# Softmax denominators of a local-attention kernel: a column of ones in the value tile and a vector shuffle in place of matmuls with ones

## Chip, cores, metric

The kernel runs on one core of a Trainium2 chip. The metric is the device time of one execution in microseconds (us); smaller is better. Before the change it was 201.92 us (median of 3 runs, 201.13 to 202.17).

Engines by their short names: PE is TensorE (matmuls), ACT is ScalarE (activation functions), DVE is VectorE, POOL is GpSimd.

## The reference, cut to what matters

```python
xn = _layernorm(x)                                # x: 1 x 2048 x 448, bf16
# attention over 16 heads of 28, window of 8 keys at distance 0, 2, ... 14
q, k, v = split(xn @ wqkv)
logits = einsum("bhsd,bhswd->bhsw", q, gather(k)) * 28 ** -0.5    # masked where the key lies before 0
attn = softmax(logits, axis=-1)
s = reshape(einsum("bhsw,bhswd->bhsd", attn, gather(v))) @ wo
# feed-forward on the same xn, hidden width 1792
g = silu(gelu(xn @ w1 + b1) @ w2 + b2)
return x + s * g
```

## The kernel before

Even and odd positions are handled as two sequences, which makes the window contiguous. Positions are cut into blocks of 121 queries with 128 keys. A *unit* is four blocks of one group of four heads. There are four stages `c = 0..3` of 512 positions; each has an FFN part (`ffn1_pair`) and then an attention part with four units (five in the last stage). The attention part also does the second FFN matmul of the stage (`ps_y`) and, in all but the last stage, the projections q, k and v of the next stage: that is work with which PE fills the time while a unit passes through the other engines.

```python
vw = [big.tile([P, H, 32], BF16) ...]       # per block: keys x heads x 32; 28 columns of v, 4 zero columns

def qk_unit(c, i):                          # logits of a unit, exp, mask
    ...
    for j, (g, b) in enumerate(u):
        for h in range(4):
            nc.tensor.matmul(Sp[h // 2][:, h % 2, j, 0:QW], kT[...], qT[...], start=True, stop=True)
    for p2 in range(2):
        ev = E[:, 2 * p2:2 * p2 + 2, :, 0:QW]
        nc.scalar.activation(ev, Sp[p2][:, :, :, 0:QW], ACT.Exp, scale=SCALE)
        nc.vector.tensor_tensor(out=ev, in0=ev, in1=mk..., op=ALU.mult)
    return E

def av_unit(c, i, E):                       # denominators, numerators, quotient
    psO = psB.tile([P, 4, P], F32, name="psO", tag="B")
    psD = psB.tile([P, 4, P], F32, name="psD", tag="B")
    for h in range(4):                      # denominators: 32 columns of ones, so that all 32 rows hold the sum
        nc.tensor.matmul(psD[32 * h:32 * h + 32, :, 0:QW], ones[:, :], E[:, h, :, 0:QW], start=True, stop=True)
    for j, (g, b) in enumerate(u):          # numerators
        for h in range(4):
            nc.tensor.matmul(psO[32 * h:32 * h + 32, j, 0:QW], vw[b][:, 4 * g + h, :], E[:, h, j, 0:QW],
                             start=True, stop=True)
    nc.scalar.activation(ld[:, :, 0:n], psD[:, :, 0:n], ACT.Ln)                  # 1/den as exp(-ln(den))
    nc.scalar.activation(R[:, :, 0:n], ld[:, :, 0:n], ACT.Exp, scale=-1.0)
    nc.vector.tensor_tensor(out=dst, in0=psO[:, :, 0:n], in1=R[:, :, 0:n], op=ALU.mult)   # -> oT

# order of the program; PE and ACT run exactly in this order, DVE is ordered by a scheduler
for c in range(NC):
    for k in range(MT // 2):
        ffn1_pair(c, 2 * k)                 # ps_h, then gelu on ACT, two at a time, in 2 PSUM tiles (psA)
        ...                                 # silu and output projection of earlier rows, transposes
    jobs = iter(list(qkv_jobs(c + 1))) if c + 1 < NC else iter(())
    n_units = 4 + (c == 3)
    for i in range(n_units):
        E = qk_unit(c, i)
        if i < 4:
            ffn2_job(4 * c + i)             # ps_y, then y = ps_y + b2 on DVE
        run(jobs, 3 if i < 3 else 99)       # none in the last stage
        av_unit(c, i, E)
...                                         # tail: tanh, silu, last output projections
```

The logits tiles `S` and the `ps_h` tiles share two PSUM tiles (psA); `ps_y`, `ps_qk`, `ps_v`, `psO`, `psD` and others share four PSUM buffers in rotation (psB).

The softmax here doesn't subtract the row's maximum and nothing guards it: scores larger than these inputs give would overflow.

Of the kernel before, what the change touches and what calls it, by code (L numbers as in the profile page):

```python
# [8 lines left out]
F32 = mybir.dt.float32  # L9
BF16 = mybir.dt.bfloat16  # L10
U32 = mybir.dt.uint32
ALU = mybir.AluOpType
ACT = mybir.ActivationFunctionType
ENG = mybir.EngineType

S, D, H, DH, F = 2048, 448, 16, 28, 1792
P = 128
# [6 lines left out]
QB = 121  # L24
QW = 122
# [8 lines left out]
def kernel(  # L34
# [14 lines left out]
    nc = tc.nc  # L49
# [8 lines left out]
    const = ctx.enter_context(tc.tile_pool(name="const", bufs=1))  # L58
    big = ctx.enter_context(tc.tile_pool(name="big", bufs=1))
    work = ctx.enter_context(tc.tile_pool(name="work", bufs=2))  # L60
    psA = ctx.enter_context(tc.tile_pool(name="psA", bufs=2, space=bass.MemoryType.PSUM))
    psB = ctx.enter_context(tc.tile_pool(name="psB", bufs=4, space=bass.MemoryType.PSUM))
# [6 lines left out]
    vw = [big.tile([P, H, 32], BF16, name=f"vw_{b}") for b in range(NB)]  # L69
# [8 lines left out]
    wo = big.tile([P, 4, D], BF16, name="wo")  # L78
# [2 lines left out]
    lnv = const.tile([P, NT], F32, name="lnv")  # L81
    ident = const.tile([P, P], BF16, name="ident")
    eps_t = const.tile([P, 1], F32, name="eps_t")
    ones = const.tile([P, 32], BF16, name="ones")
    b1t = const.tile([P, MT], BF16, name="b1t")
    b1f = const.tile([P, MT], F32, name="b1f")
    b2bc = const.tile([P, D], BF16, name="b2bc")
# [33 lines left out]
        nc.gpsimd.memset(tl[:, :, 0:LEAD].bitcast(U32), 0)  # L121
        nc.gpsimd.memset(tl[:, :, LEAD + S:LQ].bitcast(U32), 0)
    nc.gpsimd.memset(w1[64:128, 3, :].bitcast(U32), 0)
    nc.gpsimd.memset(ones[:], 1.0)
    for b in range(NB):
        nc.gpsimd.memset(vw[b][:, :, DH:32].bitcast(U32), 0)

    nc.gpsimd.memset(mk_gen[:, :, :], 1.0)
    nc.gpsimd.affine_select(out=mk_gen[:, :, :], in_=mk_gen[:, :, :], compare_op=ALU.is_ge, fill=0.0,
# [12 lines left out]
    for g in range(4):  # L142
        for h in range(4):
            r = (4 * g + h) * DH
            nc.gpsimd.dma_start(wo[32 * h:32 * h + DH, g, :], A_wo[r:r + DH, :])
    nc.gpsimd.tensor_copy(b1f[:], b1t[:])


# [34 lines left out]
    def v_job(b):  # L183
        ps = psB.tile([P, D], F32, name="ps_v", tag="B")
        o = LEAD + QB * b - 7
        for kt in range(KT):
            nc.tensor.matmul(ps[:, :], xnT[:, kt, o:o + P], wqkv[:, kt, 2 * D:3 * D],  # L187
                             start=(kt == 0), stop=(kt == KT - 1))
        nc.scalar.copy(vw[b][:, :, 0:DH], ps[:, :].rearrange("p (h c) -> p h c", h=H))  # L189

    def ffn1_pair(c, m0):
        ps = psA.tile([P, 2, CH], F32, name="ps_h", tag="A")
# [36 lines left out]
    def unit(c, i):  # L229
        if i < 4:  # L230
            return [(i, 4 * c + j) for j in range(4)]
        return [(g, NB - 1) for g in range(4)]

    def qk_unit(c, i):
        u = unit(c, i)
        E = work.tile([P, 4, 4, P], BF16, name="E", tag="E", bufs=2)
        Sp = [psA.tile([P, 2, 4, P], F32, name="S", tag="A") for _ in range(2)]
        for j, (g, b) in enumerate(u):
            o = LEAD + QB * b
            for h in range(4):  # L240
                r = slice(32 * h, 32 * h + DH)
                nc.tensor.matmul(Sp[h // 2][:, h % 2, j, 0:QW], kT[r, g, o - 7:o - 7 + P],  # L242
                                 qT[r, g, o:o + QW], start=True, stop=True)
# [3 lines that stand above are left out]
            mk = mk_gen if i == 4 or c % 2 else (mk_0, None, mk_8)[c]  # L247
            nc.vector.tensor_tensor(out=ev, in0=ev,  # L248
                                    in1=mk[:, :, :].unsqueeze(1).to_broadcast((P, 2, 4, QW)), op=ALU.mult)
        return E  # L250

    def av_unit(c, i, E):
        u = unit(c, i)
        psO = psB.tile([P, 4, P], F32, name="psO", tag="B")
        psD = psB.tile([P, 4, P], F32, name="psD", tag="B")
        for h in range(4):
            nc.tensor.matmul(psD[32 * h:32 * h + 32, :, 0:QW], ones[:, :], E[:, h, :, 0:QW],  # L257
                             start=True, stop=True)
        for j, (g, b) in enumerate(u):
            for h in range(4):  # L260
                nc.tensor.matmul(psO[32 * h:32 * h + 32, j, 0:QW], vw[b][:, 4 * g + h, :],  # L261
                                 E[:, h, j, 0:QW], start=True, stop=True)
        n = QB if i < 4 else S - QB * (NB - 1)
        ld = work.tile([P, 4, QB], F32, name="ld", tag="ld", bufs=2)
        R = work.tile([P, 4, QB], F32, name="R", tag="R", bufs=2)
        nc.scalar.activation(ld[:, :, 0:n], psD[:, :, 0:n], ACT.Ln)  # L266
        nc.scalar.activation(R[:, :, 0:n], ld[:, :, 0:n], ACT.Exp, scale=-1.0)  # L267
        if i < 4:
            dst = oT[:, i, 4 * QB * c:4 * QB * (c + 1)].rearrange("p (j q) -> p j q", j=4)
        else:  # L270
            dst = oT[:, :, QB * (NB - 1):S]
        nc.vector.tensor_tensor(out=dst, in0=psO[:, :, 0:n], in1=R[:, :, 0:n], op=ALU.mult)  # L272
# [3 lines left out]
    def qkv_jobs(c):  # L276
        for g in range(4):
            for which in range(2):
                yield lambda g=g, which=which: qk_job(c, g, which)
        for b in range(4 * c, 4 * c + 4 + (c == 3)):  # L280
            yield lambda b=b: v_job(b)
# [9 lines left out]
    with tc.manual_schedule(engines={ENG.PE, ENG.Activation}):  # L291
# [13 lines left out]
        for c in range(NC):  # L305
# [23 lines left out]
# [3 lines that stand above are left out]
                    ffn2_job(4 * c + i)  # L332
                run(jobs, 3 if i < 3 else 99)
                if i == 4:
                    pass
                av_unit(c, i, E)
# [36 lines left out]
```

## Time and profile before

| | before |
|---|---|
| time, median | 201.92 us |
| busy: PE, DVE, ACT | 172.6, 111.8, 117.3 of 201.3 us |
| lengths of stages 1 to 4 (see below) | 41.19, 41.95, 42.19, 23.53 us |
| last stage, from one ld to the next | 4.13 us |

How to read the stage lengths: in the timeline of ACT, every FFN part ends with a gelu pair in front of a load of the exp table. The length of a stage is the time from the start of that last gelu pair to that of the next; the fourth runs from the last such pair to the table load in front of the closing tanh. So a stage here is an attention part with the FFN part that follows it, and the fourth is the last attention part alone. The two gelu pairs that bound the first stage of the kernel before (timeline of ACT: start us, length us, engine and line, operation; in brackets the idle time before it and what ended it):

```profile
41.95 1.26 ACT L201 ACTIVATE hT<-ps_h,b1f 128x512 bf16<-128x512 f32 x2 [0.46 <-PE ps_h L196]
...
83.14 1.26 ACT L201 ACTIVATE hT<-ps_h,b1f 128x512 bf16<-128x512 f32 x2 [0.46 <-PE ps_h L196]
```

The first stage is 83.14 - 41.95 = 41.19 us long.

The busy line of the page of the kernel before, engine by engine: busy us, share of the span, number of instructions.

```profile
PE 172.6 (86%) x1384; PEld 84.1 (42%) x1384; DVE 111.8 (56%) x220; ACT 117.3 (58%) x181; POOL 16.0 (8%) x56
```

PE is busiest, but not everywhere the limit. Two pieces of the chain of waits of the kernel before (start us, length us, engine, what); the first piece is from the first stage, the second from the last stage:

```profile
49.01 0.32 PE psD L257 x4
49.32 0.21 PE psO L261 x16
...
171.75 0.68 DVE E L248
172.43 0.04 issue
172.48 0.40 PE psD L257 x2
172.90 0.58 ACT ld L266
173.50 0.61 ACT R L267
174.11 1.76 ACT E L246 x2
```

In the first stage one PE item follows another: PE is the chain, and psD is 0.32 us of it per unit. In the last stage, where no projections are left to fill PE's time, the chain goes round a ring: mask multiply, psD, ld, R, the next unit's exps. ACT runs in the order of the program, so the exps of unit i+1 stand behind ld and R of unit i, and PE and DVE wait in turn.

The groups of instructions that the change concerns, kernel before: line, engine, operation, output and inputs, shapes, count; then busy us in total and mean ns of one; then the engine's idle time just before them and what ended it:

```profile
L272 DVE TENSOR_TENSOR oT<-psO,R 128x484 bf16<-128x484 f32 x16 | 10.6, 662 | 24.5 <-ACT R L267 24.5
...
L267 ACT ACTIVATE R<-ld 128x484 f32<-128x484 f32 x16 | 9.7, 606 | 0.5
...
L266 ACT ACTIVATE ld<-psD 128x484 f32<-128x484 f32 x16 | 9.2, 576 | 22.6 <-PE psD L257 22.6
...
L257 PE MATMUL psD<-E,ones 128*32 128x488 bf16 x68 | 8.7, 384 | 3.6 <-DVE E L248 3.2
...
L261 PE MATMUL psO<-E,vw 128*32 128x122 bf16 x272 | 8.0, 222 | 0.0
```

The oT multiply is the model for a shuffle's cost: the same 484 fp32 elements per partition, read from PSUM by DVE in 662 ns. The timeline of the kernel before, in the form explained above. The first two lines are ACT and PE at the start of the second FFN part, the others ACT in the last stage:

```profile
70.21 1.26 ACT L201 ACTIVATE hT<-ps_h,b1f 128x512 bf16<-128x512 f32 x2
...
71.59 1.89 PE L196 MATMUL ps_h<-xnT,w 128*128 128x512 bf16 x8
...
172.90 0.57 ACT L266 ACTIVATE ld<-psD 128x484 f32<-128x484 f32 x1 [1.17 <-PE psD L257]
...
177.03 0.57 ACT L266 ACTIVATE ld<-psD 128x484 f32<-128x484 f32 x1 [1.18 <-PE psD L257]
```

The first gelu pair ends at 70.21 + 1.26 = 71.47 us, and the third ps_h pair, which needs the PSUM tile that this gelu frees, starts at 71.59 us. PE could not have come much earlier with profit. In the last stage ld starts every 177.03 - 172.90 = 4.13 us.

### The profile page before, as it was taken

The page shows a single profiled execution, that of the slowest core. Times are in us where ns is not written, and L with a number is a line of the kernel's source. Part 1 is how long each engine was busy: PE and PEld are TensorE (multiplying, and loading weights), DVE is VectorE, ACT ScalarE, POOL GpSimd, SP SyncE. Part 2 cuts the span into 40 slices and gives each one's busy share as a digit, 9 for nine tenths or more (in the row PEclk, how much of TensorE's full clock was granted, in tenths as well). Part 3 has the DMA queues.
Part 4 walks back from the last instruction along what each step waited for, and adds up shares of the span by engine and source line. Part 5 has one row for each costly group of instructions (what it writes and reads, how often), then busy time and mean ns, then how long its engine had stood idle before and what let it go on. Part 6 is the DMA issues. An engine that isn't in the chain of part 4 may idle for free.

```text
span 201.3 us, 3396 instructions
## 1 busy us (share of the span) xinstructions
PE 172.6 (86%) x1384; PEld 84.1 (42%) x1384; DVE 111.8 (56%) x220; ACT 117.3 (58%) x181; POOL 16.0 (8%) x56
## 2 busy tenths in 40 slices
PE   0048999979999999799999998899999997998570
PEld 0032445434455454345454543454444443444230
DVE  1886794009775356087753464377651651665494
ACT  0600057684356895745567965754469857657750
POOL 8966000000000000000000000000000000000000
PEclk9999999999999999999999999999999999999787
DMA  5999900000000001000000002000000010000002
GB/s 186 359 229 276 295 2 3 0 0 0 3 0 3 2 0 46 26 0 0 3 0 3 0 23 68 0 5 0 3 0 0 23 49 23 0 3 2 3 23 91
DMA packets 9743, 8.82 MB, mean 44 GB/s; under 512 B 2592, under 2 KB 8832, under 8 KB 9728
## 3 DMA queue, kind: packets, MB, share of 16 engines
q1 hardware_dynamic: 8704, 7.00, 12.4%
q10 hardware_dynamic: 512, 1.20, 1.6%
q0 software_dynamic: 512, 0.40, 1.0%
q8 instruction: 11, 0.18, 0.4%
q14 instruction: 4, 0.03, 0.0%
HBM read 6.77 MB, written 1.84 MB: 43 GB/s over the span
## 4 chain that ended last, share of the span: by engine, by line
PE 73%; ACT 11%; DMA 6%; DVE 6%; issue 2%; DVEq 0%
PE ps_h L196 23%; PE ps_y L207 16%; PE ps_qk L177 15%; PE ps_v L187 6%; DMA wqkv<-in_A_wqkv_dram 6%; PE ps_s L220 5%; ACT E L246 5%; ACT hT L201 3%; PE psD L257 3%; PE S L242 2%; DVE E L248 2%; PE psO L261 2%; ACT ld L266 1%; PE pT L165 1%; DVE sg L223 1%
## 5 line engine op out<-in xcount | busy, mean ns | idle before, releaser
L196 PE MATMUL ps_h<-xnT,w 128*128 128x512 bf16 x224 | 52.3, 379 | 0.2 <-ACT hT L201 0.2
L207 PE MATMUL ps_y<-w,hT 128*128 128x448 bf16 x224 | 45.2, 353 | 0.0
L201 ACT ACTIVATE hT<-ps_h,b1f 128x512 bf16<-128x512 f32 x56 | 35.4, 684 | 15.6 <-PE ps_h L196 15.5
L177 PE MATMUL ps_qk<-xnT,wqk 128*128 128x512 bf16 x128 | 32.1, 406 | 1.9 <-DVE xnT L166 1.9
L246 ACT ACTIVATE E<-S 128x976 bf16<-128x976 f32 x34 | 31.3, 973 | 0.0
L196 PEld LDWEIGHTS <-w 128*128 128x128 bf16 x224 | 21.3, 98 | 23.9 <-issue 0.5
L207 PEld LDWEIGHTS <-hT 128*128 128x128 bf16 x224 | 20.6, 98 | 19.2
L272 DVE TENSOR_TENSOR oT<-psO,R 128x484 bf16<-128x484 f32 (+1 forms) x17 | 11.2, 659 | 26.4 <-ACT R L267 26.4
L266 ACT ACTIVATE ld<-psD 128x484 f32<-128x484 f32 (+1 forms) x17 | 9.8, 574 | 24.0 <-PE psD L257 24.0
L189 ACT CAST vw<-ps_v 128x448 bf16<-128x448 f32 x17 | 9.0, 532 | 23.0 <-PE ps_v L187 23.0
L177 PEld LDWEIGHTS <-wqk 128*128 128x128 bf16 x128 | 13.1, 103 | 18.7 <-issue 3.8
L165 PE MATMUL pT<-ident,xnb 128*128 128x128 bf16 x64 | 6.7, 242 | 12.0 <-DVE xnb L159 12.0
L248 DVE TENSOR_TENSOR E<-E,mk_gen 128x976 bf16<-128x976 bf16 x18 | 12.0, 669 | 7.4 <-ACT E L246 7.4
L220 PE MATMUL ps_s<-wo,oT 128*128 128x448 bf16 x64 | 15.3, 376 | 0.0
L214 DVE SCALAR_TENSOR_TENSOR g<-th,y 128x448 bf16<-128x448 bf16 x16 | 9.8, 624 | 8.8 <-ACT th L213 8.7
L248 DVE TENSOR_TENSOR E<-E,mk 128x976 bf16<-128x976 bf16 x16 | 10.7, 668 | 7.0 <-ACT E L246 6.8
L187 PE MATMUL ps_v<-wqkv,xnT 128*128 128x448 bf16 x68 | 14.0, 352 | 0.0
L223 DVE SCALAR_TENSOR_TENSOR sg<-ps_s,g 128x448 bf16<-128x448 f32 x16 | 9.9, 622 | 7.0 <-PE ps_s L220 7.0
L159 DVE TENSOR_SCALAR xnb<-x,mv,rstd 128x448 bf16<-128x448 bf16 x16 | 5.7, 389 | 13.5 <-ACT rstd L156 13.5
L181 DVE CAST qT<-ps_qk 128x512 bf16<-128x512 f32 x16 | 11.0, 687 | 2.7 <-PE ps_qk L177 2.7
L181 DVE CAST kT<-ps_qk 128x512 bf16<-128x512 f32 x16 | 11.0, 689 | 2.1 <-PE ps_qk L177 2.0
L151 DVE BATCH_NORM_STATS2 st<-x 128x6 f32<-128x448 bf16 x16 | 9.5, 606 | 4.2 <-DMA x<-in_A_x_dram 4.2
(49 smaller groups left out, 136.2 us busy)
## 6 DMA issues: line engine op xcount, KB each, us to landing
out_dram<-o_t SPq DMA_DIRECT2D x16, 112.0 KB, 1.7
w<-in_B_w_dram SPq DMA_DIRECT2D x1, 1568.0 KB, 15.8
x<-in_A_x_dram SPq DMA_DIRECT2D x3, 448.0 KB, 8.7
w<-in_B_w_dram SPq DMA_DIRECT2D x1, 1344.0 KB, 10.3
wqkv<-in_A_wqkv_dram ACTq DMA_DIRECT2D x3, 336.0 KB, 4.5
x<-in_A_x_dram SPq DMA_DIRECT2D x4, 112.0 KB, 4.2
wo<-in_A_wo_dram POOLq DMA_DIRECT2D x16, 24.5 KB, 6.1
w<-in_B_w_dram SPq DMA_DIRECT2D x1, 224.0 KB, 10.3
```

Source lines behind the costliest of these rows:

```text
L177: nc.tensor.matmul(ps[:, :], wqk[:, kt, 16 * which + 4 * g:16 * which + 4 * g + 4, :], xnT[:, kt, LEAD + c * CH:LEAD + (c + 1) * CH], star ...
L181: nc.vector.tensor_copy(dst[:, g, LEAD + c * CH:LEAD + (c + 1) * CH], ps[:, :])
L187: nc.tensor.matmul(ps[:, :], xnT[:, kt, o:o + P], wqkv[:, kt, 2 * D:3 * D], start=(kt == 0), stop=(kt == KT - 1))
L196: nc.tensor.matmul(ps[:, i, :], w1[:, kt, m * P:(m + 1) * P], xnT[:, kt, LEAD + c * CH:LEAD + (c + 1) * CH], start=(kt == 0), stop=(kt == ...
L201: nc.scalar.activation(hT[0][:, m, :], ps[:, i, :], ACT.Gelu_apprx_tanh, bias=b1f[:, m:m + 1])
L207: nc.tensor.matmul(ps[:, :], hT[0][:, m, tt * P:(tt + 1) * P], w2[:, m, :], start=(m == 0), stop=(m == MT - 1))
L220: nc.tensor.matmul(ps[:, :], oT[:, g, t * P:(t + 1) * P], wo[:, g, :], start=(g == 0), stop=(g == 3))
L223: nc.vector.scalar_tensor_tensor(out=sg[:], in0=ps[:, :], scalar=0.5, in1=g_sb[t % 8][:], op0=ALU.mult, op1=ALU.mult)
L246: nc.scalar.activation(ev, Sp[p2][:, :, :, 0:QW], ACT.Exp, scale=SCALE)
L248: nc.vector.tensor_tensor(out=ev, in0=ev, in1=mk[:, :, :].unsqueeze(1).to_broadcast((P, 2, 4, QW)), op=ALU.mult)
L266: nc.scalar.activation(ld[:, :, 0:n], psD[:, :, 0:n], ACT.Ln)
L272: nc.vector.tensor_tensor(out=dst, in0=psO[:, :, 0:n], in1=R[:, :, 0:n], op=ALU.mult)
```

## The change

The intent: the padded value tile has four unused columns per head. If one of them holds ones, the numerator matmul yields the denominator as one of its 32 rows for nothing, and 68 matmuls with ones fall away. But the denominator then stands in one row, and the division needs it in all 32. DVE's stream shuffle, called with the selection `[0] * 32`, copies row 0 of each group of 32 rows to all 32. The column of ones is put first, so v, and the rows of wo that go with it, move by one.

```diff
-    ones = const.tile([P, 32], BF16, name="ones")
...
-    nc.gpsimd.memset(ones[:], 1.0)
     for b in range(NB):
-        nc.gpsimd.memset(vw[b][:, :, DH:32].bitcast(U32), 0)
+
+        nc.gpsimd.memset(vw[b][:, :, 0:1], 1.0)
+        nc.gpsimd.memset(vw[b][:, :, DH + 1:32], 0.0)
...
-            nc.gpsimd.dma_start(wo[32 * h:32 * h + DH, g, :], A_wo[r:r + DH, :])
+            nc.gpsimd.dma_start(wo[32 * h + 1:32 * h + 1 + DH, g, :], A_wo[r:r + DH, :])
...
-        nc.scalar.copy(vw[b][:, :, 0:DH], ps[:, :].rearrange("p (h c) -> p h c", h=H))
+        nc.scalar.copy(vw[b][:, :, 1:DH + 1], ps[:, :].rearrange("p (h c) -> p h c", h=H))
...
         psO = psB.tile([P, 4, P], F32, name="psO", tag="B")
-        psD = psB.tile([P, 4, P], F32, name="psD", tag="B")
-        for h in range(4):
-            nc.tensor.matmul(psD[32 * h:32 * h + 32, :, 0:QW], ones[:, :], E[:, h, :, 0:QW],
-                             start=True, stop=True)
...
-        nc.scalar.activation(ld[:, :, 0:n], psD[:, :, 0:n], ACT.Ln)
+        den = work.tile([P, 4, QB], F32, name="den", tag="den", bufs=2)
+        nc.vector.stream_shuffle(den[:, :, 0:n], psO[:, :, 0:n], [0] * 32)
+        nc.scalar.activation(ld[:, :, 0:n], den[:, :, 0:n], ACT.Ln)
```

## The prediction

> **What bounds the kernel now.** TensorE (PE) is busy 172.6 of 201.3 us, VectorE (DVE) 111.8, ScalarE (ACT) 117.3 (the page's busy times); the limit changes with the stage. In the chain of waits, PE is the chain in the first three attention stages (43 to 152 us): each unit adds 0.32 us of psD and 0.21 us of psO matmuls to it. At each following FFN stage the third pair of ps_h matmuls waits for ACT: in the timeline the first gelu pair ends at 71.47 us and the third matmul pair starts at 71.59: 0.1 us of slack; after the third attention stage ACT is the chain outright (vw, ld, R, table load, gelu from 151.1 to 155.4). In the last attention stage (168 to 190 us) the chain is a loop of 4.13 us per unit: two exps E 1.76, mask multiply 0.68, psD 0.42, ld 0.58, R 0.61, next exps.
>
> **What changes.** Removed: 68 psD matmuls; psO starts 0.21 us after psD in the timeline, so PE gains about 0.2 us per unit. Added: 17 shuffles on DVE, reading 484 fp32 elements from PSUM. [...] The oT multiply of this shape and source takes 0.66 us in the trace, so I estimate 0.66 to 0.77 us each, about 12 us of DVE work. Moved: ld now waits psO, then the shuffle, not psD; it reads SBUF, not PSUM (R from SBUF takes 606 ns, ld 576: +0.03 us). The value tiles' memsets double on GpSimd, long before use: no cost.
>
> **On the critical path.**
> - First three stages: PE gets about 0.2 x 4 = 0.8 us ahead per stage, but the last unit's ld now follows psO and a shuffle. By the timeline it still starts at about 67.7 us; R, table load and first gelu keep their times, and the third ps_h pair waits for them. The gain turns into a PE wait on gelu of about 0.7 us. DVE, saturated around 48 to 50 us, takes 0.7 us more per 6 us unit; masks come late in places: +0.0 to +0.3 us per stage. Together +0.3.
> - Last stage: shuffle plus hand-over enters the loop, 4.13 becoming about 4.9 to 5.1 us. Four units give +3.2 to +4.0, the fifth (448 elements, no new exps) +0.7 to +0.9. Together +4.3.
> - Tail only shifts.
>
> **Predicted time: 206.5 us, range 204.3 to 208.8 (8 in 10).** Faster by over 2%: 0.01; within: 0.37; slower: 0.62.
>
> **What would show it.** PE busy down by roughly 10 us; shuffle group x17 at 0.66 to 0.77 us; DVE busy near 123 us. In the last stage the E pairs 4.9 to 5.1 us apart instead of 4.13, ld waiting on den instead of psD (24.0 us in the waits); and a new wait of PE ps_h on ACT hT of about 0.7 us at each FFN stage's third pair. The first three stages keep their length within 0.3 us.
>
> **What would make it wrong.** A shuffle far from 0.7 us (at 0.4 us the result is within 2%). The psD matmuls costing PE more than 0.2 us per unit, while the FFN stage doesn't wait for gelu: then up to 2.5 us come back. DVE lateness of the masks compounding in stages one to three: slower than the range.

(The sum: 201.9 + 0.3 + 4.3 = 206.5 us. Of the estimate for one shuffle, the lower end, 0.66 us, is the oT multiply of the trace; the upper end, 0.77 us, was the author's estimate, which no trace showed. "Saturated" stands for 1.91 us of DVE work in the 2.00 us from 48 to 50 us of the kernel before.)

## The result, and the profile after

| | before | after |
|---|---|---|
| time, median (range) | 202.04 us (201.13 to 202.31, 4 runs) | 206.75 us (206.40 to 207.25, 4 runs) |
| stage 1 | 41.19 | 41.65 |
| stage 2 | 41.95 | 42.39 |
| stage 3 | 42.19 | 42.64 |
| stage 4 | 23.53 | 27.38 |
| last stage, from one ld to the next | 4.13 | 4.91 |

The ratio is 1.0243 (95% interval 1.0204 to 1.0282): slower by 2.4%. A ratio here is the mean time of one kernel's fast runs over the mean time of the other's fast runs of the same rounds, so it is not quite the ratio of the medians quoted.

The stages grew by 0.46 + 0.44 + 0.45 + 3.85 = 5.20 us in the two profiled executions; the medians differ by 4.71 us. The profiled execution of before happened to have a late start: its first stage began at 41.95 us, that of the changed kernel at 40.73 us. A second profile of the unchanged kernel (below) began it at 39.77 us with the same stage lengths, so this gap belongs to the execution and not to the change. The first stage of the changed kernel lies between these two gelu pairs, 82.38 - 40.73 = 41.65 us:

```profile
40.73 1.27 ACT L201 ACTIVATE hT<-ps_h,b1f 128x512 bf16<-128x512 f32 x2 [0.46 <-PE ps_h L196]
...
82.38 1.27 ACT L201 ACTIVATE hT<-ps_h,b1f 128x512 bf16<-128x512 f32 x2 [0.46 <-PE ps_h L196]
```

The busy line of the page, changed kernel:

```profile
PE 167.9 (82%) x1299; PEld 82.4 (40%) x1316; DVE 121.6 (59%) x254; ACT 117.9 (57%) x181; POOL 17.7 (9%) x72
```

PE fell by 4.7 us and DVE rose by 9.8 us; neither number is the answer. (The trace has 1299 matmul records where it should have 1316, 68 fewer than before; the others are missing from the record, which makes PE's fall look larger than it is.)

One round of the ring in the last stage, in the chain of waits of the changed kernel:

```profile
171.88 0.67 DVE E L248
172.55 0.50 DVE y L209
173.05 0.69 DVE den L263
173.76 0.61 ACT ld L264
174.40 0.61 ACT R L265
175.01 1.75 ACT E L246 x2
```

The shuffle (den) stands between the numerators and ld. In this round the psO matmuls finish under the cover of the y addition, which DVE does meanwhile, so they don't appear; den, the shuffle, adds its whole length. The groups, changed kernel, in the form shown above (its lines are numbered differently: psO is L257 here):

```profile
L263 DVE STREAM_SHUFFLE den<-psO 128x484 f32<-128x484 f32 x16 | 11.1, 695 | 0.0
...
L264 ACT ACTIVATE ld<-den 128x484 f32<-128x484 f32 x16 | 9.7, 606 | 35.2 <-DVE den L263 35.2
...
L257 PE MATMUL psO<-E,vw 128*32 128x122 bf16 x272 | 8.3, 224 | 8.7 <-DVE E L248 8.1 <-DVE y L209 0.7
```

A shuffle takes 695 ns, 33 ns more than the oT multiply of the same shape, and ld takes 606 ns in place of 576 now that it reads SBUF (R, which reads SBUF at the same shape, takes 606 ns in both kernels). The waits of the changed kernel (engine and what waited, for whom: us in total, times, longest us):

```profile
ACT ld L264 <- DVE den L263: 37.3, 17, 4.0
...
PE psO L257 <- DVE E L248: 8.1, 9, 3.3
...
PE ps_h L196 <- ACT hT L201: 2.4, 3, 1.1
...
PE psO L257 <- DVE y L209: 0.7, 2, 0.3
```

The 24.0 us that ld waited for psD before have become 37.3 us of waiting for den. PE, the busiest engine, now waits on DVE for masks (8.1 us, against 3.2 us in front of psD before; all of it in the last stage) and for y (0.7 us), and on ACT's gelu (2.4 us at three places, 0.2 us at one place before). The timeline of the changed kernel; the first two lines are PE around the end of the first stage, then three of DVE ahead of it, then ACT in the last stage:

```profile
65.78 0.40 PE L257 MATMUL psO<-E,vw 128*32 128x122 bf16 x16 [0.33 <-DVE y L209]
...
70.83 1.89 PE L196 MATMUL ps_h<-xnT,w 128*128 128x512 bf16 x8 [0.65 <-ACT hT L201]
...
60.77 0.70 DVE L263 STREAM_SHUFFLE den<-psO 128x484 f32<-128x484 f32 x1
...
64.53 0.67 DVE L248 TENSOR_TENSOR E<-E,mk 128x976 bf16<-128x976 bf16 x1 [0.20 <-ACT E L246]
65.11 0.62 DVE L209 TENSOR_TENSOR y<-ps_y,b2bc 128x448 f32<-128x448 f32 x1
...
173.76 0.61 ACT L264 ACTIVATE ld<-den 128x484 f32<-128x484 f32 x1 [1.92 <-DVE den L263]
...
178.68 0.61 ACT L264 ACTIVATE ld<-den 128x484 f32<-128x484 f32 x1 [1.92 <-DVE den L263]
```

The last unit's psO of the first stage waits 0.33 us for y, and the third ps_h pair waits 0.65 us for gelu. In the last stage ld starts every 178.68 - 173.76 = 4.92 us, and ACT's idle time in front of ld is 1.92 us in place of 1.17.

### The profile page after: what moved, and what is told of

Its sections match the earlier page's. It is cut to its first block, busy times and chain, and to the rows that moved or that the text cites. A ratio compares the mean times of both kernels' runs of the same rounds, so it can differ in the third digit from the quotient of the medians.

```text
span 205.0 us, 3274 instructions
## 1 busy us (share of the span) xinstructions
PE 167.9 (82%) x1299; PEld 82.4 (40%) x1316; DVE 121.6 (59%) x254; ACT 117.9 (57%) x181; POOL 17.7 (9%) x72
## 4 chain that ended last, share of the span: by engine, by line
PE 34%; ACT 29%; DVE 29%; issue 4%; DMA 2%; SPq 0%; DVEq 0%
PE ps_h L196 19%; ACT E L246 9%; DVE den L263 6%; PE ps_qk L177 6%; DVE E L248 5%; ACT ld L264 5%; ACT R L265 5%; ACT hT L201 4%; PE ps_s L220 4%; DVE y L209 4%; DVE qT L181 3%; DVE kT L181 3%; DMA x<-in_A_x_dram 2%; PE ps_v L187 2%; ACT L320 2%
## 5 line engine op out<-in xcount | busy, mean ns | idle before, releaser
L196 PE MATMUL ps_h<-xnT,w 128*128 128x512 bf16 x216 | 51.5, 379 | 2.9 <-ACT hT L201 2.4
L177 PE MATMUL ps_qk<-xnT,wqk 128*128 128x512 bf16 x119 | 30.7, 399 | 2.3 <-DVE xnT L166 1.9
L264 ACT ACTIVATE ld<-den 128x484 f32<-128x484 f32 (+1 forms) x17 | 10.3, 605 | 37.3 <-DVE den L263 37.3
L220 PE MATMUL ps_s<-wo,oT 128*128 128x448 bf16 x64 | 16.2, 393 | 0.0
L257 PE MATMUL psO<-E,vw 128*32 128x122 bf16 x272 | 8.3, 224 | 8.7 <-DVE E L248 8.1
```

What stands on the lines that cost most here:

```text
L177: nc.tensor.matmul(ps[:, :], wqk[:, kt, 16 * which + 4 * g:16 * which + 4 * g + 4, :], xnT[:, kt, LEAD + c * CH:LEAD + (c + 1) * CH], star ...
L196: nc.tensor.matmul(ps[:, i, :], w1[:, kt, m * P:(m + 1) * P], xnT[:, kt, LEAD + c * CH:LEAD + (c + 1) * CH], start=(kt == 0), stop=(kt == ...
L220: nc.tensor.matmul(ps[:, :], oT[:, g, t * P:(t + 1) * P], wo[:, g, :], start=(g == 0), stop=(g == 3))
L264: nc.scalar.activation(ld[:, :, 0:n], den[:, :, 0:n], ACT.Ln)
```

## Experiments

The theory to test: the shuffle costs as *latency*, wherever a chain of dependent steps runs through it (the ring of the last stage, and the end of each earlier stage). The rival: it costs as *occupancy* of DVE, which is about 10 us busier, wherever it stands. All kernels gave the right result except the one that is wrong on purpose. Kernels of one heading ran on the same chip and share the runs of the kernel before. Stage lengths of all runs, us:

| kernel | ratio to before (95%) | stage 1 | 2 | 3 | 4 |
|---|---|---|---|---|---|
| before | 1 | 41.19 | 41.95 | 42.19 | 23.53 |
| changed | 1.0243 (1.0204 to 1.0282) | 41.65 | 42.39 | 42.64 | 27.38 |
| before_again | 0.9985 (0.9948 to 1.0022) | 41.19 | 41.95 | 42.20 | 23.52 |
| shuffle_first3 | 1.0071 (1.0041 to 1.0100) | 41.65 | 42.39 | 42.64 | 23.52 |
| shuffle_last | 1.0168 (1.0143 to 1.0193) | 41.19 | 41.95 | 42.19 | 27.38 |
| dead_shuffle | 1.0003 (0.9973 to 1.0033) | 41.20 | 41.95 | 42.19 | 23.53 |
| no_den (wrong) | 0.9930 (0.9898 to 0.9962) | 40.60 | 41.36 | 41.66 | 24.01 |
| shuffle_unit3 | 1.0102 (1.0058 to 1.0146) | 41.81 | 42.56 | 42.87 | 23.32 |
| shuffle_units012 | 0.9975 (0.9934 to 1.0017) | 41.05 | 41.78 | 41.96 | 23.53 |
| pipe_before | 0.9827 (0.9791 to 0.9863) | 41.20 | 41.95 | 42.19 | 20.37 |
| pipe_after | 0.9923 (0.9887 to 0.9960) | 41.64 | 42.39 | 42.64 | 21.05 |
| ahead_before | 0.9991 (0.9953 to 1.0030) | 42.39 | 43.15 | 42.59 | 20.57 |
| ahead_after | 0.9843 (0.9808 to 0.9878) | 41.20 | 41.95 | 41.39 | 21.06 |
| combined | 0.9668 (0.9625 to 0.9711) | 40.37 | 41.13 | 41.00 | 19.75 |

The stage lengths repeat to 0.01 us from one execution to the next (before and before_again; the one exception is the fourth stage of shuffle_unit3, explained there), which makes them a far sharper instrument than the total time.

### Where the loss sits: four kernels on one chip

**before_again.** The kernel before, unchanged (no edit).

> The kernel before, unchanged, as a control: ratio 1.00 within 0.3%. Its profile is to show how far the start-up varies: the last gelu pair of the first FFN stage began at 41.95 us in the profile of before and at 40.73 in that of the changed kernel. If that 1.2 us belongs to the single execution and not to the change, this run can show a value near 41 as well; if it stays at 41.95, the change itself shortened the start-up.

Measured: 201.45 us, ratio 0.9985; the last gelu pair of the first FFN part began at 39.77 us, the stage lengths are those of before. The start-up varies with the execution and says nothing about the change.

**shuffle_first3 and shuffle_last.** The layout of the changed kernel throughout, and in each stage one or the other source of the denominators:

```diff
         psO = psB.tile([P, 4, P], F32, name="psO", tag="B")
+        shuffled = c < 3                 # shuffle_last: c == 3
+        if not shuffled:
+            psD = ...                    # and the four matmuls with ones, as before
...
+        if shuffled:
             nc.vector.stream_shuffle(den[:, :, 0:n], psO[:, :, 0:n], [0] * 32)
             nc.scalar.activation(ld[:, :, 0:n], den[:, :, 0:n], ACT.Ln)
+        else:
+            nc.scalar.activation(ld[:, :, 0:n], psD[:, :, 0:n], ACT.Ln)
```

> Shuffle in the first three attention stages, matmuls with ones in the last. Latency theory (the shuffle costs where it stands in a chain of dependent steps): the last stage's loop is back at 4.13 us per unit, the first three stages keep their +0.45 us each, so before + 1.35 us, about 203.3 us, ratio 1.005 to 1.008. Rival, occupancy of VectorE (each shuffle costs its share of the 4.7 us wherever it stands): 12 of 17 shuffles, so +3.3 us, about 205.3 us, ratio 1.016.

Measured: 203.58 us, ratio 1.0071; the first three stages as in the changed kernel, the fourth as in the kernel before. The timeline of ACT in its last stage:

```profile
173.71 0.57 ACT L275 ACTIVATE ld<-psD 128x484 f32<-128x484 f32 x1 [1.17 <-PE psD L261]
...
177.85 0.57 ACT L275 ACTIVATE ld<-psD 128x484 f32<-128x484 f32 x1 [1.18 <-PE psD L261]
```

From one ld to the next 4.14 us, and the idle time before ld is back at 1.17 us.

> Matmuls with ones in the first three attention stages, shuffle in the last alone. Latency theory: loop of 4.91 us per unit in the last stage, the first three as before, so +3.7 to +3.9 us, about 205.8 us, ratio 1.018 to 1.020. Occupancy rival: 5 of 17 shuffles, so +1.4 us, about 203.4 us, ratio 1.007.

Measured: 205.17 us, ratio 1.0168, a little under the expected 1.018, which lies inside the interval. The fourth stage is that of the changed kernel, 27.38 us. Its timeline there:

```profile
171.98 0.61 ACT L273 ACTIVATE ld<-den 128x484 f32<-128x484 f32 x1 [1.92 <-DVE den L272]
...
176.89 0.61 ACT L273 ACTIVATE ld<-den 128x484 f32<-128x484 f32 x1 [1.92 <-DVE den L272]
```

What follows: the two losses are separate and add up (0.71% + 1.68% = 2.39% against 2.43%). Five shuffles of the last stage cost 3.85 us, twelve of the first three 1.35 us. Per shuffle that is 0.77 us against 0.11 us, so the cost goes by place and not by number. The occupancy rival had expected the opposite proportion. (The 0.11 us are net of what PE gains in these stages; no_den, below, puts that gain at 1.71 us, and (1.35 + 1.71) / 12 = 0.26 us is then the price of a shuffle there. In the last stage no_den finds no gain to set off.)

**dead_shuffle.** The kernel before, with the same 17 shuffles added, but nobody reads them:

```diff
+        den = work.tile([P, 4, QB], F32, name="den", tag="den", bufs=2)
+        nc.vector.stream_shuffle(den[:, :, 0:n], psO[:, :, 0:n], [0] * 32)
         nc.scalar.activation(ld[:, :, 0:n], psD[:, :, 0:n], ACT.Ln)
```

> The kernel before with all 17 shuffles added, their result read by nobody; the denominators still come from matmuls with ones. Latency theory: VectorE is as busy as in the changed kernel (about 122 us), but no step waits for the shuffle, so the last stage's loop stays at 4.13 to 4.3 us and the time at 202.0 to 203.0 us, ratio 1.000 to 1.005. Occupancy rival: all of the cost, about 206.5 us, ratio 1.02.

Measured: 201.93 us, ratio 1.0003. The busy line of its page:

```profile
PE 171.5 (86%) x1384; PEld 83.7 (42%) x1384; DVE 123.2 (61%) x254; ACT 117.4 (59%) x181; POOL 15.9 (8%) x56
```

Its timeline in the last stage, ACT and then DVE:

```profile
171.83 0.57 ACT L268 ACTIVATE ld<-psD 128x484 f32<-128x484 f32 x1 [1.18 <-PE psD L257]
...
175.97 0.57 ACT L268 ACTIVATE ld<-psD 128x484 f32<-128x484 f32 x1 [1.17 <-PE psD L257]
...
172.06 0.70 DVE L267 STREAM_SHUFFLE den<-psO 128x484 f32<-128x484 f32 x1
```

DVE is even busier than in the changed kernel (123.2 against 121.6 us), a shuffle is as long (0.70 us), and all four stages keep their lengths to 0.01 us. This refutes the occupancy rival as stated, a cost of every shuffle wherever it stands: the same 17 shuffles go with a loss of 4.7 us where ld waits for them and with none where nobody does. It does not say that DVE's queue never matters: in this run PE had no lead that late DVE work could eat, and two places below show a step that waits behind other work on DVE.

### Where PE's gain went in the first three stages

The changed kernel saves PE 0.21 us per unit, and still each early stage is 0.45 us longer. Three kernels on one chip take this apart.

**no_den.** The matmuls with ones removed and nothing put in their place.

```diff
-        den = work.tile([P, 4, QB], F32, name="den", tag="den", bufs=2)
-        nc.vector.stream_shuffle(den[:, :, 0:n], psO[:, :, 0:n], [0] * 32)
-        nc.scalar.activation(ld[:, :, 0:n], den[:, :, 0:n], ACT.Ln)
+        nc.scalar.activation(ld[:, :, 0:n], psO[:, :, 0:n], ACT.Ln, bias=eps_t[:], scale=0.0)
```

> Wrong result on purpose: the changed kernel without the shuffle, ld reading psO directly (scaled by zero, so that no logarithm of a negative value arises). It shows what taking the 68 matmuls away is worth when nothing is put in their place. My theory: PE leads by 0.2 us per unit, ld of the last unit of a stage starts about 0.6 us earlier, so the first three stages shorten by 0.4 to 0.6 us each; the last stage's loop stays within 0.1 us of 4.13. Total -1.0 to -1.8 us, ratio 0.991 to 0.995. Rival, the matmuls sit wholly on the critical path (0.32 us per unit in the chain, 0.42 in the last stage): -5 us, ratio 0.975. Other rival, they are hidden: ratio 1.000.

Measured: 200.25 us against 201.44 us for the kernel before of the same rounds, ratio 0.9930. Removing all 68 matmuls at no cost is worth 0.59 + 0.59 + 0.53 us in the first three stages. The fourth got 0.48 us longer, which is an artefact of the replaced ld, as the timeline of ACT there shows:

```profile
170.47 0.66 ACT L262 ACTIVATE ld<-psO,eps_t 128x484 f32<-128x484 f32 x1 [1.18 <-PE psO L257]
```

The idle time before ld is 1.18 us, the same as with psD, but this ld with its bias operand takes 0.66 us in place of 0.57: 0.09 us in each of five units. In the last stage, then, waiting for the numerators is no longer than waiting for the matmuls with ones, and removing the latter gains nothing there. So a shuffle that is to break even in this order of the program may cost 1.7 us in the whole kernel.

**shuffle_unit3 and shuffle_units012.** The conditional of shuffle_first3 again, within the first three stages:

```diff
-        shuffled = c < 3
+        shuffled = c < 3 and i == 3      # shuffle_units012: c < 3 and i < 3
```

> In the first three stages the shuffle stands in the last unit of the stage alone (all other units, and the last stage, use matmuls with ones). If the stage's end (psO, shuffle, ld, R, table load, gelu, third ps_h pair) is what costs, each of these stages gets about 0.5 to 0.65 us longer than before (41.19, 41.95, 42.19 us), as PE has gained nothing in units 0 to 2. If instead late masks in units 0 to 2 are the cost, the stages keep their length within 0.15 us.

Measured: 203.80 us, ratio 1.0102; the first three stages are 0.62, 0.61 and 0.68 us longer than before. (The fourth is 0.21 us shorter, although its code is that of before: the idle time in front of the last ld is 1.17 in place of 1.38 us. In the kernel before, the last matmuls with ones are the slowest of their group, up to 587 ns against a median of 380, after PE had waited 2.3 us. The profiles show a slower granted clock with it: in the microsecond of these matmuls and of psO it was 0.52 of full speed in the kernel before (189 to 190 us), and on the page of shuffle_unit3 it is 0.9 or more in the slice that holds them (187.1 to 192.2 us). Why it differs is not shown; the change of code lies in other stages.)

> In the first three stages the shuffle stands in units 0 to 2, matmuls with ones in the last unit. If the stage's end alone costs, PE's lead of 0.6 us survives and these stages get 0.1 to 0.6 us shorter. If VectorE's backlog and the late masks eat the lead, they keep their length within 0.15 us, and PE shows a wait of 0.2 to 0.5 us on VectorE before the last unit's psD or psO. The sum of the changes of this run and of the one with the last unit alone should be near the +0.45 us per stage of the full change.

Measured: 201.29 us, ratio 0.9975; the first three stages are 0.14, 0.17 and 0.23 us shorter. The two runs' changes add up to +0.48, +0.44 and +0.45 us, against +0.46, +0.44 and +0.45 of the full change. A line from the waits of shuffle_units012:

```profile
PE psD L261 <- DVE y L211: 0.7, 2, 0.3
```

What follows: the last unit's shuffle costs 0.6 us at the stage's end, where psO, shuffle, ld, R, the table load (1.28 us) and the first gelu follow each other and the third ps_h pair waits for that gelu. Against it stands PE's lead from units 0 to 2, which should be 3 x 0.21 = 0.63 us; of it only 0.14 to 0.23 us arrive, where no_den, without shuffles, gained 0.53 to 0.59. The waits say where it goes in the first two stages: PE waits for y in front of the last unit's psD (and, in the changed kernel, 0.33 us in front of psO, whose PSUM buffer is the one that y frees). The timeline of the changed kernel, above, has the cause a step further back: the shuffle of unit 2 starts at 60.77 us, behind a queue of DVE work, and so the second mask of unit 3 comes at 64.53 and y only at 65.11. Counted from the start of the stage, the value projections of unit 3 still start on PE at 22.29 us in the changed kernel, against 22.83 before, a lead of 0.54 us; then y starts at 24.38 us, against 23.42 before, and with the wait for it the lead ends. The scheduler also put y between the two masks of units 1 and 2 on DVE in the changed kernel, where it had followed them; how much of the lateness is due to that order, how much to the shuffle's own length and how much to the queue is not separated here.

### Taking the latency off the chain: four kernels on one chip

If the shuffle costs only as latency, the order of the program should be able to hide it.

**pipe_before and pipe_after.** The kernel before and the changed kernel, with the logits and exps of unit i+1 issued ahead of the denominators of unit i, in the last stage alone:

```diff
+            else:                                   # c == 3
+                E = qk_unit(c, 0)
+                for i in range(n_units):
+                    if i < 4:
+                        ffn2_job(4 * c + i)
+                    E_next = qk_unit(c, i + 1) if i + 1 < n_units else None
+                    av_unit(c, i, E)
+                    E = E_next
```

> The kernel before with one change of order in the last attention stage: the logits and exps of unit i+1 are issued ahead of the denominators of unit i, so the loop E, mask, psD, ld, R is no longer closed over one unit. The loop should then be bound by TensorE (S 0.33, ps_y 2.75, psD and psO 0.53: about 3.6 us) instead of 4.13 us. Over four units -1.5 to -2.2 us, about 200 us, ratio 0.989 to 0.993.

Measured: 198.51 us, ratio 0.9827, a larger gain than expected: the fourth stage is 3.16 us shorter. The first ld comes 1.01 us later there, as the exps of unit 1 now go first; the next three gaps between ld's give 1.13 us, and the gap to the last ld falls from 4.34 to 1.29 us, because the last unit's exps are done by then. That last term I had left out. Two successive exp pairs of ACT in its last stage:

```profile
178.86 1.86 ACT L246 ACTIVATE E<-S 128x976 bf16<-128x976 f32 x2 [0.66 <-PE S L242]
...
182.47 1.86 ACT L246 ACTIVATE E<-S 128x976 bf16<-128x976 f32 x2 [0.65 <-PE S L242]
```

3.61 us apart, and they wait for S, which is PE.

> The changed kernel with the same change of order in the last stage. If the shuffle costs only as latency, its 0.7 us vanish from the loop: 3.4 to 3.6 us instead of 4.91, over four units -5.2 to -6.0 us against the changed kernel; what stays is +1.35 us of the first three stages and the last unit's shuffle. About 201 us, ratio to before 0.993 to 1.000. If VectorE's throughput were the cost, the loop would stay above 4.5 us and the ratio above 1.012.

Measured: 200.28 us, ratio 0.9923. The same two pairs:

```profile
178.93 1.86 ACT L246 ACTIVATE E<-S 128x976 bf16<-128x976 f32 x2 [0.43 <-PE S L242]
...
182.34 1.86 ACT L246 ACTIVATE E<-S 128x976 bf16<-128x976 f32 x2 [0.42 <-PE S L242]
```

3.41 us apart in place of 4.91. The gain on the changed kernel's fourth stage, 27.38 - 21.05 = 6.33 us, is a little more than the 5.2 to 6.0 us expected. The shuffle is no shorter, but it has left the ring, and here the removed matmuls show at last: 3.61 - 3.41 = 0.20 us per unit. The fourth stage is still 0.68 us longer than that of pipe_before (21.05 against 20.37), because the very last unit's shuffle has nothing to hide behind: ld waits 1.32 us for it. About half of that is DVE's queue, by an estimate from the timelines: the last psO matmuls end at 185.34 us and ld starts at 186.65, 1.31 us later, of which the shuffle of the last unit (448 elements) takes 0.67 us in the changed kernel; R of the unit before ends at 185.33 us, and the oT multiply that it releases takes 0.66 us, about the rest. The first three stages, not touched, keep their +0.45 us each.

**ahead_before and ahead_after.** The same idea in all stages; in the first three the value projections come first, and two query and key projections are left for after the last unit's psO:

```diff
-            jobs = iter(list(qkv_jobs(c + 1))) if c + 1 < NC else iter(())
+            todo = list(qkv_jobs(c + 1)) if c + 1 < NC else []
+            jobs = iter(todo[8:] + todo[:8])
...
+            E = qk_unit(c, 0)
             for i in range(n_units):
-                E = qk_unit(c, i)
                 if i < 4:
                     ffn2_job(4 * c + i)
-                run(jobs, 3 if i < 3 else 99)
+                E_next = qk_unit(c, i + 1) if i + 1 < n_units else None
+                run(jobs, 3 if i < 3 else 1 + (c == 2))
                 av_unit(c, i, E)
+                E = E_next
+            run(jobs, 99)
```

> The kernel before with units issued one ahead in all four stages, and in the first three the value projections moved to the front so that two query and key projections follow the last unit's psO. Last stage as in the run with the order changed in that stage alone; the first three gain little, as TensorE bounds them: -0.1 to -0.4 us each. About 199.5 us, ratio 0.984 to 0.992.

Measured: 201.68 us, ratio 0.9991. This expectation failed: the first three stages got 1.20, 1.20 and 0.40 us longer and ate what the last stage gained. PE, which bounds these stages in this kernel, starts the second FFN part 1.21 us later after the start of the stage than in the kernel before. The waits that the trace names for it are 0.28 us at the start of the stage, where the second set of S matmuls comes before the exps of the first have freed their PSUM tile, and 0.32 us in front of the last ps_y, for a copy of kT. Most of the rest can be read from the timeline of PE: three times a stage S now follows ps_y directly and starts 2.76 us after it, where ps_qk started 2.66 us after it before, together 0.3 us; and the second S set, cut in two by the wait, takes about 0.2 us more.

> The changed kernel with the same order. The shuffle is off every chain, so the removed matmuls should at last show: 0.2 us per unit of TensorE time against the other kernel of this order, so 1 to 2.5 us faster than it. About 197.8 us, ratio to before 0.975 to 0.985. If it is not faster than the kernel before in this order by at least 0.5 us, the shuffle still costs as much as the matmuls even when hidden.

Measured: 198.62 us, ratio 0.9843, at the edge of the expected range (the time expected was 197.8): the first two stages are only as long as in the kernel before, and the same 0.28 us wait for the exps is there. Yet in this order the change is a gain: 198.62 against 201.68 us, 1.5% faster than the same order with matmuls with ones. The 3.06 us are more than the 1 to 2.5 us expected. Each of the first three stages is 1.2 us shorter than in ahead_before: about 0.84 us are four times PE's 0.21 us, and most of the rest is the wait in front of the last ps_y (0.32 us in the first stage), which is gone. Nothing that ps_y computes with comes from kT; it waits for a PSUM buffer. Counted through the program, the last ps_y gets the buffer of the second query or key projection of the unit before when psD takes its turn in the rotation of four, and the buffer of the first, which is free sooner, when psD is gone. So the change has a second benefit in this order, a buffer that is freed; no run tests it by itself.

### A version that beats both

**combined.** The shuffle in every unit but the very last, which keeps the matmuls with ones because nothing can hide its shuffle; and the S matmuls of unit i+1 moved behind the projections, right in front of psO of unit i:

```diff
-        shuffled = c < 3
+        shuffled = not (c == 3 and i == 4)
...
-                E_next = qk_unit(c, i + 1) if i + 1 < n_units else None
                 run(jobs, 3 if i < 3 else 1 + (c == 2))
+                E_next = qk_unit(c, i + 1) if i + 1 < n_units else None
                 av_unit(c, i, E)
```

> A version meant to beat both: the shuffle in every unit except the very last one of the last stage (where nothing can hide it), the logits and exps of unit i+1 issued just ahead of the denominators of unit i in all stages, value projections first, and two query and key projections after the last psO of the first three stages. From the stage lengths measured so far: the last stage 19.6 to 20.4 us instead of 23.53, the first three 0.4 to 0.8 us shorter each. About 196.3 us, ratio to before 0.966 to 0.977. If the first three stages don't shorten, the ratio stays near 0.98 and the gain comes from the last stage alone.

Measured: 195.38 us (194.34 to 195.86, 6 runs) against 202.10 us, ratio 0.9668 (0.9625 to 0.9711): 3.3% faster than the kernel before. All four stages are shorter. The timeline at the start of its second FFN part, ACT and PE:

```profile
68.05 1.27 ACT L203 ACTIVATE hT<-ps_h,b1f 128x512 bf16<-128x512 f32 x2
...
69.83 1.89 PE L198 MATMUL ps_h<-xnT,w 128*128 128x512 bf16 x8
```

The first gelu pair ends at 68.05 + 1.27 = 69.32 us and the third ps_h pair starts at 69.83 us without a wait: ACT is ahead of PE there by 0.5 us. Against ahead_after, which has the same shuffles in the first three stages, these stages are 0.83, 0.82 and 0.39 us shorter, and that is the place of S alone; the fourth is 1.31 us shorter with matmuls with ones in the last unit. What the shuffle contributes was not run with matmuls with ones in exactly this order; the pairs above suggest that it contributes too.

## Why the prediction was right, and where it was not

The time (206.75 us against a predicted 206.5) and the direction were right, and so was the reason: the removed matmuls lie where they are worth little, and the shuffle lies in a ring. But the sum came out partly by luck: two of its terms were off in opposite directions (+1.35 us in place of +0.3, +3.85 in place of +4.3), and the medians, with their varying start-up, differ by 4.71 us where the stages grew by 5.20.

- **The shuffle's length**: predicted 0.66 to 0.77 us, measured 0.695 us. The trace's own multiply of the same shape (0.662 us) is the lower end; the upper end was the author's estimate and not read from a trace. The measured surplus over the multiply is 0.033 us.
- **"Last stage: shuffle plus hand-over enters the loop, 4.13 becoming about 4.9 to 5.1 us"**: right. The ring is 4.91 us. The whole stage: predicted +4.3, measured +3.85 us. It is 4 x 0.78 + 0.74: for a full unit, ACT's idle time before ld grew by 0.75 us and ld by 0.03; for the last one, by 0.71 and 0.03.
- **"The gain turns into a PE wait on gelu of about 0.7 us"**: right in two stages (0.65 us in the first), 1.11 us in the third, where PE had already waited 0.22 us before.
- **"By the timeline it still starts at about 67.7 us ... +0.0 to +0.3 us per stage. Together +0.3"**: the step that failed. Measured from the start of the stage, the last unit's ld started at 67.68 - 41.95 = 25.73 us before and 66.96 - 40.73 = 26.23 us after. The early stages grew by 0.46, 0.44 and 0.45 us, 1.35 together. I had counted PE's lead in full (0.8 us, which was to pay for psO and the shuffle in front of the last unit's ld) and the lateness of DVE as an afterthought. The runs show that of the lead of units 0 to 2 only 0.14 to 0.23 us arrive. The prediction named the mechanism, masks that come late, but mis-sized it; what PE then waits for is y, which stands behind these masks on DVE.
- **"PE busy down by roughly 10 us"**: wrong, it fell by 4.7 us (even less, as records are missing). The page gives the psD group 8.7 us, but part of that time overlaps with other matmuls: the four psD matmuls of a unit take 0.39 us together, hardly more than one (0.38), and psO starts 0.21 us after them, which makes 17 x 0.21 = 3.6 us. The 0.21 us per unit, on which the predicted time rested, was right.
- **"DVE busy near 123 us"**: 121.6 us.
- **"The value tiles' memsets double ... no cost"**: 34 memsets in place of 17, the last of which ends at 5.9 us in the changed kernel, where the first copy into a value tile starts at 25.5 us. shuffle_last has these memsets and the stage lengths of before in its first three stages, so they cost nothing there. A cost within the 2 us by which the start-up varies was not looked for.

## What to carry to other kernels

A step that is moved from a busy engine to an idle one is not free when something waits for it: ask which chain runs through it, and not which engine has room. The same 17 shuffles cost nothing when nobody waited for them, 0.77 us each in a ring that closes within one unit, and on average 0.26 us each, of which PE's gain paid 0.14, where other work covered most of it; once the order of the program let the next unit run ahead, the change turned from a loss of 2.4% into a gain of 1.5% against the same order. Nor did it pay much here to relieve the busiest engine of the page: PE is busy for 86% of the span, and yet taking 68 matmuls off it, with nothing in their place, was worth 0.7% (no_den).

## What else the traces show

- The shuffle's length: fp32 from PSUM, 695 ns for 484 elements and 666 for 448, against 662 and 623 for a two-tensor multiply of the same shapes. So the surplus is 33 to 43 ns (5 to 7%) at these lengths.
- In front of each of the 17 shuffles the trace of the changed kernel has a DVE instruction LOAD_MASK_SELECT, 14 to 18 ns each, although the selection never changes in this kernel.
- Moving ld from PSUM to SBUF at 484 elements made it 30 ns longer (576 to 606 ns).
- The start-up: the first 32 ps_qk matmuls took between 8.52 and 9.93 us in the six profiles in which they were read (before, changed, before_again, shuffle_first3, shuffle_last, dead_shuffle). In the kernel before they took the longest, 9.93 us, at a granted clock of 1.00; why they differ is not shown. This and an earlier or later first ps_qk matmul (14.96 us in before_again, 15.97 in before) moved the start of the first stage by 2.2 us between two profiles of one kernel (39.77 and 41.95 us), 1% of the time and more than some of the effects studied here; comparing stage lengths, which repeat to 0.01 us, is how this document gets round it.
